# Local attention with v blocks of 80 keys, zero columns around K^T, and new numbers for the issue order

## The chip, the core and the metric

The kernel runs on one core of one Trainium2 chip. A core has five engines that run side by side: TensorE (PE, matrix products; its weight loads are listed as PEld), VectorE (DVE), ScalarE (ACT), GpSimd (POOL) and SyncE (SP), which here only issues transfers. Sixteen DMA engines carry the transfers. The metric is the time of one execution in device microseconds; before the change the median of three runs is 770.74 us (768.55 to 772.76).

## The reference

Two parts. The first is an attention with two terms, over q, k, v of 8 batches, 8 heads, 576 positions and 64 dimensions, in float32:

```python
q_d, k_d, v_d = means over 4 neighbours          # 144 positions instead of 576
out_up = repeat(softmax(q_d k_d^T / 8) v_d, 4)   # the coarse term
mask = |pos_i - pos_j| < 4
out_local = softmax(where(mask, q k^T / 8, -1e9)) v   # each query sees at most 7 keys
x = (out_up + out_local), as 4608 rows of 512
```

The second is a mixture of 8 experts over these 4608 rows: logits `x @ w_gate`, a greedy assignment by sorted logits with at most 576 rows for an expert, then `relu(x w1[e]) w2[e]` for each expert's rows. The change touches the first part alone.

## The kernel before

**Stages.** Stage one computes the attention and the logits. It takes the first 284 us of the profiled span and writes x to DRAM. Stage two finds the fullest expert, gathers its rows, multiplies, and repeats for eight experts. Stage two needs every logit, so it starts when the last unit of stage one has its logits.

**Units.** The local term is worked in 36 units of 128 queries (`u`), each of four windows of 32 queries; a window looks at 38 keys (`KW`), from three before its first query to three behind its last. `loc_s` (L436) makes the scores of a unit on TensorE, one 32x38 product for each window and head, on top of the mask that a first product put there (L428). VectorE takes the maximum and subtracts it (L444, L445), ScalarE makes the exponentials (L446) into a tile `sw` of 64 columns for each head, whose columns 38 to 63 are zero. `loc_t` transposes on TensorE (L454): the two windows of a pair then lie one above the other, the even window's keys on partitions 0 to 63 and the odd window's on 64 to 127. ScalarE copies both halves into the weight tile `pt` (L465, two copies of 64 partitions). `loc_v` (L476) multiplies `pt` with the keys' values `vw`, one product of 128 keys by 64 queries for each pair and head; `norm` (L404 to L407) divides on VectorE. `log_a` (L484) adds the coarse term, `log_t` and `log_m` (L494 to L514) make the logits `lg`.

**Values.** `load_vw` (L229) fills `vw`, one of four buffers: for each window 48 rows of v (`VR`) with all 8 heads, 256 bytes for each row and head. Window 0 of a pair goes to partition 0 and up, window 1 to partition 64 and up, so the six keys that two neighbours share are loaded twice, and 10 more rows come along each time. A window at the end of a batch takes two transfers, of 32 and 6 rows.

**Keys.** The transposed keys `kt` are 576 columns; a window at either end of a batch is pushed inwards (`key0` clamps) and its mask differs.

**The coarse term.** For each batch: `trw` and `trt` transpose q and k (L292, L306), with evacuations (L276 on VectorE, L278 on ScalarE) that `EV` deals out, one in five to VectorE after the first 29 (`EN0`), which alternate. `gsum` makes the sums over four (L265, L268). `down_s`, `down_t`, `down_v` are its scores, transposes and products; its results go to DRAM (`up_dram<-xu`, L387) and come back by `load_up` with each row four times (`up<-up_dram`, L416), which waits until the write has landed.

**What sets the order.** `run` gives every piece a place on one scale, in units, and sorts: `LOC` holds the places of a unit's pieces behind its number, `TW` and `TWS` those of a batch's transposes, `DW` and `DWS` those of its coarse term, `NEXT` those of the loads of a later batch (`q0`, `k0`: the first four heads, `q1`, `k1` the other four, `t` the tail, `v0`, `v1`). The sorted list is what each engine runs, in that order, with no reordering. All loads and stores of stage one go through SP's queue, so a transfer that must wait holds back every later one. `FL`, `FT`, `FD` say how many pieces later some ScalarE and VectorE work is issued. `SETUP` and `SPACE` place the preparation of the routing between the units (L828 to L857).

## Time and profile before

| | before |
|---|---|
| median of three runs | 770.74 us |
| the profiled execution, its own time | 767.14 us |
| its span, first to last instruction | 765.1 us |
| PE busy in the span | 671.1 us (88%) |
| PEld | 464.0 us (61%) |
| DVE | 549.7 us (72%) |
| ACT | 332.8 us (43%) |
| POOL | 235.4 us (31%) |
| mean granted TensorE clock | 0.952 |

The time of the profiled execution is 2.0 us above its span, since the time also holds what lies outside the first and last instruction. Busy shares are means over both stages; stage one is the one to read here, and the windows view gives its share.

### The profile page before, as it was taken

How to read it: one execution, taken by the hardware profiler on the slowest of the kernel's cores; microseconds unless marked ns; L12 is line 12 of the kernel's file. 1: busy time of each engine (PE TensorE's matmuls, PEld its weight loads, DVE VectorE, ACT ScalarE, POOL GpSimd, SP SyncE). 2: the span in 40 equal slices, each digit the busy share in tenths (PEclk: the TensorE clock that was granted, in tenths of full speed). 3: DMA queues.
4: the chain of work that ended last, by engine and by line, in shares of the span. 5: the costliest groups of instructions: out<-in, count | busy, mean ns of one | idle time of the engine just before them, and what ended most of it. 6: DMA issues, size and time to landing. Idle time of an engine off the chain costs nothing.

```text
span 765.1 us, 21134 instructions
## 1 busy us (share of the span) xinstructions
PE 671.1 (88%) x8545; PEld 464.0 (61%) x8545; DVE 549.7 (72%) x1635; ACT 332.8 (43%) x632; POOL 235.4 (31%) x280
## 2 busy tenths in 40 slices
PE   6788998996998963499889799999899999999994
PEld 4667786885877851365356357467466475674852
DVE  4997887887787886788869879899879354361210
ACT  3447766575675540442425325234334244352210
POOL 8173574535436450300400412140220412202011
PEclk9999999998999985599999999999999999999998
DMA  9978999897999750712825645490947733404001
GB/s 283 182 196 243 253 203 255 210 259 222 239 249 233 188 179 1 239 44 93 259 56 221 145 142 183 87 319 2 276 130 264 218 99 114 119 2 106 19 27 35
DMA packets 152900, 126.17 MB, mean 165 GB/s; under 512 B 96996, under 2 KB 127204, under 8 KB 152804
## 3 DMA queue, kind: packets, MB, share of 16 engines
q1 hardware_dynamic: 145424, 103.30, 50.0%
q0 software_dynamic: 6432, 20.98, 8.8%
q8 instruction: 68, 1.11, 0.6%
q10 hardware_dynamic: 948, 0.55, 0.3%
q14 instruction: 28, 0.23, 0.1%
HBM read 95.30 MB, written 21.23 MB: 152 GB/s over the span
## 4 chain that ended last, share of the span: by engine, by line
issue 31%; DVE 24%; PE 22%; DMA 9%; ACT 6%; POOL 5%; SPq 1%; POOLq 0%; ACTq 0%; DVEq 0%
PE pH L1109 4%; PE pX L1138 4%; POOL out_dram L1146 3%; DMA nat<-in_q_dram 2%; DVE cmp L709 2%; PE g L476 2%; PE pR L735 2%; POOL xg L1073 2%; DVE x L407 2%; PE g L292 1%; DMA xt<-xs 1%; ACT pt L465 1%; DMA up_dram<-xu 1%; DVE x L484 1%; ACT qz L278 1%
## 5 line engine op out<-in xcount | busy, mean ns | idle before, releaser
L1109 PE MATMUL pH<-xt,wh 128*128 128x256 f16 (+1 forms) x1024 | 194.5, 288 | 4.7 <-DMA xt<-xs 3.2
L1138 PE MATMUL pX<-wh,ht 128*128 128x512 f16 (+1 forms) x640 | 180.3, 382 | 0.0
L1109 PE MATMUL pH<-xt,wl 128*128 128x320 f16 (+1 forms) x512 | 146.9, 287 | 0.0
L1138 PEld LDWEIGHTS <-ht 128*128 128x128 f16 (+1 forms) x960 | 81.0, 100 | 90.2 <-issue 5.8
L1146 POOL DMA_INDIRECT out_dram<-y,idx x40 | 41.4, 1034 | 276.4 <-ACT y L1143 252.6
L1138 PE MATMUL pX<-wl,ht 128*128 128x512 f16 (+1 forms) x320 | 118.6, 382 | 0.0
L1109 PEld LDWEIGHTS <-wh 128*128 128x128 f16 x1024 | 97.9, 98 | 33.0 <-issue 8.5
L1122 ACT ACTIVATE ht<-pH 128x512 f16<-128x512 f32 (+1 forms) x128 | 45.5, 407 | 117.3 <-PE pH L1109 112.8
L1058 DVE SCALAR_TENSOR_TENSOR wl<-nat,wh 128x512 f16<-128x512 f32 x128 | 85.3, 684 | 2.5 <-ACT wh L1056 0.3
L1125 DVE SCALAR_TENSOR_TENSOR ht<-pH,ht 128x512 f16<-128x512 f32 (+1 forms) x128 | 52.5, 450 | 34.6 <-ACT ht L1122 34.0
L1073 POOL DMA_INDIRECT xg<-x_dram,idx x40 | 42.1, 1053 | 113.3 <-DVE idx L1009 57.6
L1143 ACT ACTIVATE y<-pX 128x512 f32<-128x512 f32 (+1 forms) x40 | 23.8, 594 | 115.7 <-PE pX L1138 71.1
L1056 ACT ACTIVATE wh<-nat 128x1024 f16<-128x1024 f32 x64 | 66.9, 1056 | 6.2 <-DMA nat<-in_moe_w_dram 6.0
L1109 PEld LDWEIGHTS <-wl 128*128 128x128 f16 x512 | 50.2, 98 | 13.0 <-issue 0.6
L465 ACT COPY pt<-g 64x512 f32<-64x512 f32 x72 | 41.7, 579 | 35.5 <-PE g L454 34.3
L1093 DVE SCALAR_TENSOR_TENSOR xs<-xg,xs 128x512 f16<-128x512 f32 (+1 forms) x35 | 23.6, 688 | 45.3 <-ACT xs L1092 44.9
L292 PE MATMUL g<-ident,nat 128*128 128x128 f32 x256 | 40.4, 292 | 8.6 <-DMA nat<-in_k_dram 3.9
L476 PE MATMUL g<-vw,pt 128*64 128x65 f32 x1152 | 45.0, 229 | 2.9 <-ACT pt L465 1.2
L476 PEld LDWEIGHTS g<-vw,pt 128*64 128x64 f32 x1152 | 40.0, 142 | 9.8 <-ACT pt L465 6.2
L278 ACT COPY kt<-g 64x512 f32<-64x512 f32 (+1 forms) x53 | 33.3, 628 | 25.7 <-PE g L292 13.6
L265 POOL TENSOR_TENSOR gtmp<-qz 64x576 f32<-64x576 f32 x28 | 32.0, 1142 | 30.6 <-DVE kdt L268 22.8
L499 DVE SCALAR_TENSOR_TENSOR xt<-g,xt 128x512 f16<-128x512 f32 x36 | 24.6, 685 | 20.2 <-ACT xt L498 20.0
(223 smaller groups left out, 1163.6 us busy)
## 6 DMA issues: line engine op xcount, KB each, us to landing
nat<-in_moe_w_dram SPq DMA_DIRECT2D x28, 1024.0 KB
vw<-in_v_dram SPq DMA_DIRECT2D x136, 96.0 KB
up<-up_dram SPq DMA_DIRECT2D x36, 256.0 KB
x_dram<-x SPq DMA_DIRECT2D x36, 256.0 KB
nat<-in_q_dram SPq DMA_DIRECT2D x16, 512.0 KB
nat<-in_k_dram SPq DMA_DIRECT2D x16, 512.0 KB
nat<-in_v_dram SPq DMA_DIRECT2D x14, 512.0 KB
up_dram<-xu SPq DMA_DIRECT2D x16, 128.0 KB
```

The costliest lines, as they stand in the source:

```text
L278: self.nc.scalar.copy(out, in_)
L292: nc.tensor.transpose(p[:, a, :, fp], src[:, 4 * hh + 2 * a + s, 2 * fp:2 * fp + 2].rearrange("p f d -> p (f d)"), self.ident)
L465: self.nc.scalar.copy(out, in_)
L476: nc.tensor.matmul(o[64 * i:64 * i + 64, 65 * h:65 * h + 65], pt[:, 2 * g + i, h].rearrange("p b q -> p (b q)"), self.vw[u % 4][:, i, 4 * ...
L1056: nc.scalar.activation(hi, r, AF.Copy, scale=sc)
L1058: nc.vector.scalar_tensor_tensor(lo[:, a:a + LOP], r[:, a:a + LOP], sc, hi[:, a:a + LOP], op0=OP.mult, op1=OP.subtract)
L1073: self.fetched = nc.gpsimd.indirect_dma_start(out=xg[:n], out_offset=None, in_=self.x, in_offset=bass.IndirectOffsetOnAxis(ap=idx[:n, c:c ...
L1109: mm = nc.tensor.matmul(p[:, s, :s1 - s0], w[d][a][:, 128 * f:128 * f + 128], xt[:, b, d, s0:s1], start=j == 0, stop=j == len(seq) - 1)
L1122: last = nc.scalar.activation(hi, q, AF.Relu)
L1125: nc.vector.scalar_tensor_tensor(lo, q, 0.0, hi, op0=OP.max, op1=OP.subtract)
L1138: nc.tensor.matmul(p[o:o + m], ht[:, f, h0:h0 + m], w[4 + f // 2][b][:, 512 * (f % 2):512 * (f % 2) + 512], start=j < parts, stop=j >= len ...
L1146: i = nc.gpsimd.indirect_dma_start(out=self.out, in_=y[:n], in_offset=None, out_offset=bass.IndirectOffsetOnAxis(ap=idx[:n, c:c + 1], axis=0))
```

## The change

`load_vw` loads 80 rows for a pair of windows instead of 48 for each; the first block of a batch starts three rows later, the last one is two transfers of 64 and 3 rows. The odd window's keys therefore begin 32 rows below the even window's, and `loc_t` puts them there: its second half is copied to partitions 32 to 95 in two copies of 32 partitions, so three copies on ScalarE instead of two. The rest of `pt` stays zero. `kt` gets three zero columns at each end, in two fixed tiles (`ktp`); `key0` no longer clamps, and the mask excludes the columns outside. The warm-up's tile `wm` now lies in `pt`'s second buffer.

The numbers of the order are new throughout, among them `NEXT`, `TW`, `LOC`, `EV` (one evacuation in four to VectorE instead of one in five, from the 40th on) and `SPACE`.

```diff
--- before.py
+++ after.py
@@ -21,7 +21,7 @@
 QW = 32
 NW = S // QW
 KW = QW + 6
-VR = 48
+VR = 80
 G = S // 4
 
 GM = 128
@@ -32,22 +32,22 @@
 E, F = 8, 1024
 XS = 32.0
 GSN = ('k2',)
-SH1 = 0.416
+SH1 = 0.467
 EARLY = 1
-RDY = -0.651
+RDY = 0.161
 LU = 2
 LA = 3
 LT = 5
-NEXT = (('t', 1.415), ('q0', 1.792), ('k0', 2.351), ('q1', 2.948), ('k1', 2.546), ('v0', 2.861), ('v1', 3.806), ('w', 3.194))
+NEXT = (('t', 1.876), ('q0', 0.674), ('k0', 2.463), ('q1', 2.866), ('k1', 3.746), ('v0', 3.897), ('v1', 3.863), ('w', 3.133))
 FD = 6
 FN = 1
-FL = 7
-FT = 1
+FL = 4
+FT = 0
 PEL = ("s0", "s1", "t", "v0", "v1", "lt", "lm")
-TW = (0.129, 2.439)
-DW = (-0.791, 2.251)
-DWS = {0: (1.96, 3.4), 7: (0.089, 2.426), 2: (0.305, 2.813), 3: (-0.72, 2.467), 1: (-0.345, 2.276), 5: (-0.673, 2.314)}
-LOC = {'up': 1.406, 'st': 4.773, 't': 1.331, 'lm': 7.406, 's0': 0.33, 's1': 0.334, 'lt': 5.423, 'v0': 1.884, 'v1': 1.885, 'add': 4.575}
+TW = (0.129, 2.617)
+DW = (-1.448, 2.214)
+DWS = {0: (1.96, 3.4), 7: (0.089, 2.426), 2: (1.251, 2.601), 3: (-0.348, 2.968), 1: (-0.345, 2.276), 5: (-0.673, 2.314), 6: (-1.824, 1.993)}
+LOC = {'up': 1.395, 'st': 4.914, 't': 1.331, 'lm': 7.649, 's0': 0.33, 's1': 0.334, 'lt': 5.417, 'v0': 1.718, 'v1': 1.803, 'add': 4.664}
 GS1 = ''
 GS0 = 'qk'
 GW = 2
@@ -56,31 +56,31 @@
 UB = 3
 XB = 6
 NPT = 2
-PEV = (0,0)
-EV = (0, 0, 0, 0, 1)
+PEV = (0, 0, 0)
+EV = (0, 0, 0, 1)
 ADDU = 27
 DX = 0
 SETUP = {25:0,35:26}
-SPACE = 0.371
+SPACE = 0.253
 GS = 32.0
-VWT = 1.785
-T0 = (-1.703, 0.95)
-LD0 = (-2.849, -3.627, -0.654, -0.8, 0.549)
-LD1 = (0.094, -1.118, -0.846, -0.839, -0.245, 0.414, 2.297, 2.161)
-TWS = {1: (1.746, 2.94), 6: (0.447, 2.327)}
-E0 = -0.295
-E1 = 2.863
-UE = 31
-CE = 0.101
+VWT = 1.976
+T0 = (-1.695, 2.143)
+LD0 = (-3.332, -4.99, -0.667, -0.921, 0.832)
+LD1 = (0.255, -1.073, -1.273, -0.839, -0.661, 0.459, 1.648, 2.161)
+TWS = {1: (1.853, 2.764), 6: (0.536, 2.453), 3: (-0.024, 2.685)}
+E0 = -3.356
+E1 = 4.638
+UE = 35
+CE = 0.554
 NWARM = 13
 EV0 = (0, 1)
-EN0 = 29
+EN0 = 39
 TB = 3
-SUM0 = (1.042, 1.417, 1.097)
+SUM0 = (0.827, 1.133, 2.137)
 
 
 def key0(w):
-    return min(max(QW * w - 3, 0), S - KW)
+    return QW * w - 3
 
 
 def ukind(u):
@@ -106,15 +106,13 @@
         self.ident, ident = ident
         identh = cst.tile([128, 130 + H], BF, name="identb")
         self.identb, self.half, self.own8 = identh[:, :128], identh[:, 128:130], identh[:, 130:]
-        self.wm = cst.tile([128, 128], BF, name="wm")
-        nc.vector.memset(self.wm, 1.0)
         self.mask = cst.tile([128, 4, 4 * KW], BF, name="mask")
         self.wgf = cst.tile([128, 4, E], F32, name="wgf")
         self.wg16 = cst.tile([128, 4, 2, E], F16, name="wg16")
         for t, src in ((self.ident, ident), (identh, identb), (self.mask, maskc)) + tuple(more):
             nc.scalar.dma_start(t, src)
         self.wg = wg
-        self.vw, self.vd, self.qz, self.qdz, self.qdt, self.sw, self.ptw = [], [], [], [], [], [], []
+        self.vw, self.vd, self.qz, self.qdz, self.qdt, self.sw, self.ptw, self.ktp = [], [], [], [], [], [], [], []
         self.sd = cst.tile([128, 9, G], F32, name="sd")
         self.sdt = cst.tile([128, 2 * H, GT], F32, name="sdt")
         for i in range(2):
@@ -123,12 +121,15 @@
 
 
             self.vd.append(cst.tile([128, 2, H, D + 1], F32, name=f"vd{i}"))
+            self.ktp.append(cst.tile([128, HP, S + 6], F32, name=f"kt{i}"))
         for i in range(4):
             self.vw.append(cst.tile([128, 2, H, D + 1], F32, name=f"vw{i}"))
         for i in range(NSW):
             self.sw.append(cst.tile([128, H, 64], F32, name=f"sw{i}"))
         for i in range(NPT):
             self.ptw.append(cst.tile([128, 4, 4, 2, QW], F32, name=f"pt{i}"))
+        self.wm = self.ptw[1][:, 0, 0].rearrange("p b q -> p (b q)").bitcast(BF)
+        nc.vector.memset(self.wm, 1.0)
 
     def gate(self):
         nc = self.nc
@@ -152,6 +153,9 @@
             heads(nc.vector, nc.vector, self.qdt[0])
             for t in self.vd:
                 nc.vector.memset(t[:, 0, :, D:], 1.0)
+            for t in self.ktp:
+                nc.vector.memset(t[:, :, :3], 0.0)
+                nc.vector.memset(t[:, :, S + 3:], 0.0)
             for t in self.sw:
                 nc.gpsimd.memset(t[:, :, KW:], 0.0)
             nc.gpsimd.memset(self.ptw[0], 0.0)
@@ -220,14 +224,13 @@
     def load_vw(self, u):
 
         nc, src = self.nc, self.v
-        for c in range(4):
-            b, w = divmod(4 * u + c, NW)
+        for c in range(2):
+            b, w = divmod(4 * u + 2 * c, NW)
             k0 = key0(w)
 
-            for r0, n in ((0, VR),) if k0 + VR <= S else ((0, 32), (32, KW - 32)):
-                p0 = 64 * (c % 2) + r0
+            for r0, n in ((3, VR),) if w == 0 else ((0, VR),) if k0 + VR <= S else ((0, 64), (64, 3)):
                 nc.sync.dma_start(
-                    self.vw[u % 4][p0:p0 + n, c // 2, :, :D],
+                    self.vw[u % 4][r0:r0 + n, c, :, :D],
                     bass.AP(tensor=src.tensor, offset=src.offset + (b * H * S + k0 + r0) * D,
                             ap=[[D, n], [S * D, H], [1, D]]))
 
@@ -279,7 +282,7 @@
 
     def dest(self, b):
         if b not in self.kt:
-            self.kt[b] = self.wk.tile([128, HP, S], F32, name="kt")
+            self.kt[b] = self.ktp[b % 2][:, :, 3:3 + S]
         return self.kt[b]
 
     def trw(self, b, which, hh, s):
@@ -434,7 +437,7 @@
             for a in range(4):
                 h = 4 * g + a
                 nc.tensor.matmul(sv[32 * a:32 * a + 32, 4 * g + c], self.qz[b % 2][:, h // 2, h % 2, QW * w:QW * w + QW],
-                                 self.kt[b][:, h // 2, key0(w):key0(w) + KW], start=False, stop=True,
+                                 self.ktp[b % 2][:, h // 2, QW * w:QW * w + KW], start=False, stop=True,
                                  skip_group_check=True, tile_position=(0, 32 * a))
         if g == 0:
             return
@@ -454,9 +457,9 @@
             nc.tensor.transpose(p[:, 128 * i:128 * i + 128], t[:, 2 * i:2 * i + 2].rearrange("p h k -> p (h k)"),
                                 self.ident)
         out = self.ptw[u % NPT]
-        for a in range(2):
-            r = slice(64 * a, 64 * a + 64)
-            self.pevac(a, out[r, :, :, a], p[r].rearrange("p (i h q) -> p i h q", h=4, q=QW))
+        for j, (a, r0, n) in enumerate(((0, 0, 64), (1, 64, 32), (1, 96, 32))):
+            d0 = r0 - 32 * a
+            self.pevac(j, out[d0:d0 + n, :, :, a], p[r0:r0 + n].rearrange("p (i h q) -> p i h q", h=4, q=QW))
 
     def pevac(self, a, out, in_):
         if PEV[a]:
@@ -1234,7 +1237,8 @@
         for c in range(4):
             w = (4 * u + c) % NW
             d = QW * w + p[:, None] % QW - key0(w) - np.arange(KW)[None]
-            m[kind, c][np.abs(d) < 4] = 0.0
+            k = key0(w) + np.arange(KW)[None]
+            m[kind, c][(np.abs(d) < 4) & (k >= 0) & (k < S)] = 0.0
     base, at = [], -32768
     for (_, step), (n, nxt) in zip(LV, LV[1:] + ((1, 0),)):
         at -= step
```

What the new numbers move is shown at three places. Lines of the new kernel stand three lower down from `load_nat` on, so L229 becomes L232 and L465 becomes L468.

SP's queue, around the results of the third batch's coarse term (`xu`); `nat` are the loads of q, k and v for a later batch. Before:

```order
L387 DMA up_dram<-xu 128x256
L394 DMA up_dram<-xu 8x16x64
L215 DMA nat<-in_k_dram 128x4x256
L487 DMA x_dram<-x 128x512
L416 DMA up<-up_dram 128x1x512 x2
L215 DMA nat<-in_v_dram 128x4x256
L215 DMA nat<-in_q_dram 128x4x256
L206 DMA natw<-in_v_dram 128x1x256
L229 DMA vw_129<-in_v_dram 48x8x64 x4
L416 DMA up<-up_dram 128x1x512
L487 DMA x_dram<-x 128x512
L215 DMA nat<-in_v_dram 128x4x256
```

After:

```order
L219 DMA nat<-in_k_dram 128x4x256
L419 DMA up<-up_dram 128x1x512 x2
L219 DMA nat<-in_q_dram 128x4x256
L490 DMA x_dram<-x 128x512
L232 DMA vw_129<-in_v_dram 80x8x64 x2
L210 DMA natw<-in_v_dram 128x1x256
L419 DMA up<-up_dram 128x1x512
L219 DMA nat<-in_k_dram 128x4x256
L219 DMA nat<-in_v_dram 128x4x256 x2
L490 DMA x_dram<-x 128x512
```

The second half of q stood behind half of v and stands ahead of it now; the second half of k stood ahead of the two `up` loads and stands behind three of them; both halves of v are last.

ScalarE, the last units of stage one. Before:

```order
L446 ACTIVATE sw_131<-sw_131 128x8x38
L465 COPY pt_133<-g 64x16x32 x2
L498 ACTIVATE xt<-g 128x512
L446 ACTIVATE sw_132<-sw_132 128x8x38
L465 COPY pt_134<-g 64x16x32 x2
L498 ACTIVATE xt<-g 128x512 x5
```

After:

```order
L449 ACTIVATE sw_131<-sw_131 128x8x38
L468 COPY pt_133<-g 64x16x32
L468 COPY pt_133<-g 32x16x32 x2
L501 ACTIVATE xt<-g 128x512
L449 ACTIVATE sw_132<-sw_132 128x8x38
L468 COPY pt_134<-g 64x16x32
L468 COPY pt_134<-g 32x16x32 x2
L501 ACTIVATE xt<-g 128x512 x5
```

The copies into `pt` are three where they were two; what stands around them is the same.

VectorE, the preparation of the routing between the last units (`am`, `oh`). Before:

```order
L444 TENSOR_REDUCE mx<-g 128x8
L445 TENSOR_TENSOR sw_132<-g,mx 128x8x38
L850 TENSOR_REDUCE am<-eq 128x26
L514 TENSOR_REDUCE lg<-g 128x8
L499 SCALAR_TENSOR_TENSOR xt<-g,xt 128x512
L857 TENSOR_TENSOR oh<-eq,amu 128x8x26
L404 TENSOR_SCALAR den<-g 128x4
L405 RECIPROCAL den<-den 128x4
L407 TENSOR_TENSOR x<-g,den 128x256
```

After:

```order
L853 TENSOR_REDUCE am<-eq 128x26
L407 TENSOR_SCALAR den<-g 128x4
L408 RECIPROCAL den<-den 128x4
L410 TENSOR_TENSOR x<-g,den 128x256
L407 TENSOR_SCALAR den<-g 128x4
L408 RECIPROCAL den<-den 128x4
L410 TENSOR_TENSOR x<-g,den 128x256
L860 TENSOR_TENSOR oh<-eq,amu 128x8x26
L447 TENSOR_REDUCE mx<-g 128x8
```

`am` and `oh` stood behind the last unit's scores (`mx`, `sw`); they stand ahead of them now, about a unit earlier.

## The prediction

> **What bounds the kernel now.** I read the windows view first, to see where the span goes and which stage the edited lines are in, then who waited for whom, then the chain of waits, then groups, transfers and the timeline of single places.
>
> The windows view: start:end, length, busy us of PE, PEld, DVE, ACT and POOL with instructions, granted clock, share of the DMA engines, GB/s.
>
> ```profile
> 0.00:284.00 284.00, 244.70 (x5164) 202.35 (x5165) 230.73 (x620) 170.13 (x333) 150.32 (x198) 0.96 0.89 228
> 120.00:130.00 10.00, 7.50 (x147) 6.42 (x144) 6.71 (x17) 8.50 (x18) 3.28 (x4) 0.94 0.98 249
> 130.00:140.00 10.00, 9.76 (x196) 8.47 (x196) 7.94 (x23) 5.39 (x10) 3.14 (x6) 0.89 0.93 213
> 180.00:190.00 10.00, 5.17 (x103) 3.97 (x101) 6.16 (x16) 5.38 (x13) 3.94 (x5) 0.84 0.79 231
> 190.00:200.00 10.00, 10.00 (x176) 9.15 (x175) 4.98 (x14) 6.79 (x13) 2.43 (x3) 0.82 1.14 300
> 220.00:230.00 10.00, 8.55 (x198) 7.41 (x197) 7.64 (x23) 9.73 (x21) 0.00 (x0) 1.00 1.12 277
> 284.00:765.00 481.00, 426.40 (x3384) 261.61 (x3383) 318.92 (x1016) 162.62 (x299) 85.10 (x82) 0.95 0.43 128
> ```
>
> Stage one, the attention, is 284 us; the other 481 us hold none of the edited lines and stay. In stage one PE is busy for 86%, DVE for 81%, the DMA engines for 89%: three resources near their limit, none at it throughout. So a saving on one counts only where that one is late, and two windows show where: in 120 to 130 and 180 to 190 both PE and DVE sit idle. The waits (total us, times, longest) of the attention name the cause:
>
> ```profile
> PE g L306 <- DMA natt<-in_k_dram: 4.6, 2, 3.9
> PE g L292 <- DMA nat<-in_k_dram: 3.9, 2, 3.3
> PE g L292 <- DMA nat<-in_q_dram: 3.2, 3, 2.3
> DVE x L484 <- DMA up<-up_dram: 2.6, 3, 1.7
> PEld g L476 <- ACT pt L465: 6.2, 14, 0.9
> ```
>
> The chain of waits (start, length, what) shows how the two idle stretches come about:
>
> ```profile
> 113.38 4.45 DMA up_dram<-xu
> 117.84 0.56 SPq L416
> 118.46 0.60 SPq L416
> 119.11 0.59 SPq L215
> 119.73 8.35 DMA nat<-in_q_dram
> 128.22 0.63 PE g L292 x4
> ...
> 177.75 5.92 DMA up_dram<-xu
> 183.74 0.56 SPq L416
> 184.34 4.22 DMA nat<-in_k_dram
> 188.69 1.09 PE g L292 x4
> ```
>
> A write of the coarse term must land before SP may issue the loads that read it back; the next batch's q or k is queued behind, lands 4.2 to 8.4 us later, and PE waits for it. These are stalls of the transfer path, and they cost clock too: 0.89 and 0.82 in the windows after them.
>
> **What the change takes off the transfers.** Before, a batch's windows bring 17 x 48 + 38 = 854 rows of v; now 8 x 80 + 67 = 707. Times 8 heads and 8 batches that is 9,408 packets of 256 bytes fewer, 2.41 MB. SP issues 152 transfers for them before, by the view of the tile `vw`, and 80 now:
>
> ```profile
> L229 SPq DMA_DIRECT2D vw<-in_v_dram x152: 311/466/2377, 12.8 to 266.5; - x152
> q1 hardware_dynamic: 100272, 63.57, 86.8%
> q1 hardware_dynamic: 4673, 2.07, 80.3%
> ```
>
> At the median of 466 ns the 72 issues are 33.6 us of SP's time. The two `q1` rows (packets, MB, share of 16 engines) are SP's queue in 0 to 285 us and in 250 to 260 us, where 4,156 of the packets are under 512 bytes. The first gives 0.868 x 285 x 16 / 100,272 = 39.5 ns for a packet, or by bytes 3,958 us x 2.41 / 63.57; the second 0.803 x 160 / 4,673 = 27.5 ns. So the saving of queue time is between 150 / 16 = 9.4 us by bytes and 9,408 x 39.5 ns / 16 = 23.2 us by mean packets. I take 16.2 us from the second row, whose packets are the kind that goes. That is a twentieth of the queue's time, spread over the stage.
>
> **What of it reaches the end.** At most what the stalls cost: idle PE in the two windows, 2.5 + 4.8 = 7.3 us; lost clock, 7.50 x 0.06 + 9.76 x 0.11 + 5.17 x 0.16 + 10.00 x 0.18 = 4.2 us; DVE's waits for `up`, 2.6 us; together 14.1 us. At least nothing, if another wait stands right behind. The 4.6 us for the first `natt` stay, since nothing ahead of it in SP's queue changes. Both stalls open with a transfer, and the reordering helps the first: q's second half, late at 119.73, no longer stands behind half of v. It doesn't help the second, where k's first half still stands behind the `up` loads. I take 9 us, nearer the upper end. That order can also cost is the third rival.
>
> A rule of the skill bears on the clock part. The Trainium skill, "TensorE: Matmul & The Clock Gate", section "What's actually happening", says that an idle window of some 3.4 us throttles the PE clock to half and that about as much sustained work restores it. The trace agrees in kind, with 0.84 and 0.82 around the wait of some 4 us. By that rule a stall cut below the window would give back the whole 4.2 us, and the term would be some 11 us instead of 9.
>
> **What it adds on ScalarE and VectorE.**
>
> ```profile
> L465 ACT COPY pt<-g 64x512 f32<-64x512 f32 x72 | 41.7, 579 | 35.5 <-PE g L454 34.3
> L278 ACT COPY kt<-g 64x512 f32<-64x512 f32 x46 | 28.9, 627 | 14.2 <-PE g L292 13.6
> L276 DVE COPY qz<-g 64x512 f32<-64x512 f32 x26 | 17.9, 689 | 2.5 <-PE g L292 2.1
> ```
>
> The 36 more copies into `pt` have as many elements for each partition, so I take the same 579 ns: 20.8 us of ACT. `EV` moves 11 evacuations from ACT to DVE: 11 x 627 ns = 6.9 us off ACT, 11 x 689 ns = 7.6 us onto DVE. Net ACT +13.9 us, DVE +7.6 us. Most of this is covered: ACT is busy for 60% of the stage, and where it is full, as in 220 to 230 (9.73 of 10), DVE has slack (7.64), which is where evacuations happen. If DVE's cover were gone all 7.6 us would show; I take 1 us. The zero columns are four small memsets behind a memset of 2 us; the last POOL memset of `pt` must now wait for the warm-up, whose products end at 1.21 + 5.24 = 6.45 us, 0.25 us after it is due, and POOL idles 0.64 us later on for the first v:
>
> ```profile
> 1.21 5.24 PE L617 MATMUL g<-wm 128*128 128x512 bf16 x13 [1.21 <-DVE wm L110]
> 6.20 0.95 POOL L160 MEMSET pt<- 128x1024 f32 x1
> 15.64 1.27 POOL L241 TENSOR_TENSOR gtv<-nat 128x512 f32<-128x512 f32 x1 [0.64 <-DMA nat<-in_v_dram]
> ```
>
> So nothing for these. What isn't covered is the delay of `pt` itself. One unit at the end of the stage, from the timeline:
>
> ```profile
> 266.47 0.66 PE L454 MATMUL g<-ident,sw 128*128 128x128 f32 x4
> 267.22 1.18 ACT L465 COPY pt<-g 64x512 f32<-64x512 f32 x2 [1.64 <-PE g L454]
> 268.45 1.22 PE L476 MATMUL g<-vw,pt 128*64 128x65 f32 x32
> ```
>
> The value products start 0.05 us after the second copy. PE has about 1.3 us of other work between (scores, logits, a transpose of x), just enough for two copies, not for three. So such a unit grows by nearly 0.58 us. In the new order nine units after the first have only this work between `loc_t` and `loc_v`, among them the last four; before it was 15, so the order makes room elsewhere. Upper bound 9 x 0.58 = 5.2 us, lower bound the last four, 2.3 us, where nothing else is left to do. I take 3.5 us.
>
> **The end of stage one.** Two steps of the routing's preparation stand on DVE among the last units:
>
> ```profile
> 272.30 0.50 DVE L850 TENSOR_REDUCE am<-eq 128x26 f32<-128x208 bf16 x1
> 273.45 0.97 DVE L857 TENSOR_TENSOR oh<-eq,amu 128x208 bf16<-128x208 bf16 x1
> ```
>
> DVE runs without a gap there until the last unit is normalized. Moved a unit ahead, to where PE will be waiting for the third copy, they leave up to 1.4 us; I take 1 us, nothing being the other end.
>
> **Sum.** -9 + 1 + 3.5 - 1 = -5.5 us. The profiled execution's own time is 767.14 us with a span of 765.1 us, so 761.6 and about 759.6 us now. It is 3.6 us below the median of 770.74 us, so as a median 765.2 us; I say 765.
>
> **Rivals.**
>
> *The transfers were hidden anyway.* When PE and DVE no longer wait for q and k they wait for each other: 86% and 81% busy in a chain that goes back and forth leaves little slack. For it: explicit waits for these loads are only 7.1 us. Against it: the two idle windows with both engines below 7.6 of 10. Then the transfer term is 4 us, and -4 + 1 + 3.5 - 1 leaves 770.
>
> *The 80-row block runs unevenly.* Blocks of 48 rows alternate between the lower and the upper 64 partitions; 64 of the 80 rows are in the lower half. If each half has its own way in and both halves work at once, the busier half carries 72 x 64 rows now against 72 x 48 before, a third more. v's 54,656 packets at 27.5 ns are 94 us of queue time, so +31 us instead of -16. The queue, at 86.8%, would be full, and the stalls grow: +9 in place of -9, and 783. Against it: the two queue rows price a packet by its number more than by its bytes (27.5 ns where nearly all are of 256 bytes, 39.5 ns at a mean of 634), which points at the engines and not at the ways into the memory. The Trainium skill, "SBUF — State Buffer", section "Door 1: The DMA port swizzle (why `[64,N]` ≈ `[32,N]`)", states such halves: partitions 0 to 63 reach 8 of 16 ports. No row here shows ports.
>
> *The last loads come too late; this one ends slower.* On the order's scale a load leads its first use by 4.5 plus the place of the transpose minus the place of the load. For k's first half that is 2.53 units before (4.5 + 0.386 - 2.351) and 2.44 now; for k's second half 3.62 before (4.5 + 1.669 - 2.546) and 2.54 now (4.5 + 1.788 - 3.746). A unit is 284 / 36 = 7.9 us, so the second half of k comes 8.5 us later, behind three `up` loads. It then has the lead with which the first half already waited 3.3 us. If it waits as long in three of six batches, with 2.1 us of clock each, that is 16 us; with the 9 us won and 3.5 us as above the result is 781. It decides as soon as k lands later than 2.5 units after its issue. Against it: q's halves both gain lead, and everything ahead of k in the queue is shorter.
>
> **Chances.** Forecast 0.48, with a range of its own from 758 to 769 (transfer term from 14 to 5 us); hidden transfers 0.27; late k 0.19; uneven blocks 0.06. A measurement of this kernel tells a change from none at about 0.5%, 3.9 us. Faster by more than that: nine tenths of the first case and a tenth of the second, 0.46. Slower: three quarters of the third, the fourth, and a fifth of the second, 0.25. The rest, 0.29, is no change. The range goes from 756, the whole of the stalls and a little more with an order that also closes gaps elsewhere, to 779, most of the late-k case.
>
> **What would show it.** The queue's packets in stage one should fall by 9,408 and its share to about 0.82; SP should issue 80 `vw` transfers. PE in the windows of the third and fifth coarse terms should lie above 9 of 10, and the waits of L295 (now L292) for q and k should fall below 3 us in total. The waits for `pt` on PEld should rise from 6.2 to about 10 us, and the last units should be 0.5 us longer each. I am wrong if stage one ends after 284 us: then either L295 waits for k's second half, or `pt` waits are twice what I took.

## The result, and the profile after

The changed kernel takes 776.37 us (median of 6 runs, 775.04 to 781.85) against 769.27 us of the kernel before beside it (764.84 to 772.76): a ratio of 1.011 with an interval of 1.0063 to 1.0157. It is slower, where 765 us and a small gain were forecast. Ratios here and below are taken from fast executions alone, since some executions of a kernel run in a slower state, so a ratio need not be the quotient of the two medians. Its profiled execution took 776.55 us with a span of 774.9 us.

The windows view of the changed kernel, with the columns and most of the stretches quoted of the kernel before:

```profile
0.00:284.00 284.00, 241.94 (x5161) 203.01 (x5162) 241.25 (x632) 183.15 (x358) 148.95 (x198) 0.96 0.83 219
120.00:130.00 10.00, 9.66 (x201) 7.89 (x202) 8.53 (x24) 8.10 (x19) 3.75 (x5) 1.00 1.08 295
180.00:190.00 10.00, 8.62 (x184) 7.01 (x185) 9.69 (x23) 6.11 (x15) 7.33 (x10) 1.00 0.96 256
284.00:774.00 490.00, 427.66 (x3384) 261.89 (x3383) 319.14 (x1019) 163.11 (x299) 90.19 (x82) 0.94 0.44 125
```

The two idle stretches have filled up, at full clock (7.50 and 5.17 us of PE before, at 0.94 and 0.84). Yet stage one is not shorter: the last logits of the attention end at 284.38 us, 0.51 us later than before. The other 9 us are in stage two, whose work is the same (3,384 products in both) but which now needs 490 us in place of 481. SP's queue up to 285 us (packets, MB, share of 16 engines) and SP's issues of v (shortest, median and longest in ns, first to last) show that the transfers did what was foreseen:

```profile
q1 hardware_dynamic: 89688, 61.16, 81.4%
L232 SPq DMA_DIRECT2D vw<-in_v_dram x80: 319/567/2712, 11.1 to 264.1; - x80
```

The waits of stage one (total us, times, longest) name what took their place. The k and q transposes (L295) wait 0.6 us for `nat` on PE, where it was 7.1 us, and TensorE waits for the weights and for the normalization instead:

```profile
PEld g L479 <- ACT pt L468: 9.8, 13, 1.4
PE g L479 <- ACT pt L468: 8.3, 13, 1.3
PE g L497 <- DVE den L407: 5.4, 4, 2.1
```

The groups with their shapes show the price of the third copy (count, total us, mean ns):

```profile
L468 ACT COPY pt<-g 32x512 f32<-32x512 f32 x72 | 41.6, 577 | 1.7
L468 ACT COPY pt<-g 64x512 f32<-64x512 f32 x36 | 20.8, 578 | 36.7 <-PE g L457 36.4
```

Half as many partitions cost the same time. The timeline of one of the last units, whose counterpart the prediction quotes with two copies in 1.18 us:

```profile
265.98 1.78 ACT L468 COPY pt<-g 64x512 f32<-64x512 f32 x3 [1.56 <-PE g L457]
...
267.81 1.15 PE L479 MATMUL g<-vw,pt 128*64 128x65 f32 x32 [0.74 <-ACT pt L468]
```

The value products stand still for 0.74 us.

**Where stage two loses.** Counted from the start of the first gather of x rows, the first piece `xs` of the second, third and fourth expert comes 4.5, 6.0 and 9.0 us later than before, and the end 9.3 us. So the loss arises at three places: at the first gathers, and at those of the second and third expert. The first place, on GpSimd's timeline before (start, length):

```profile
312.13 1.69 POOL L1073 DMA_INDIRECT xg<-x_dram,idx  x1 [29.37 <-DVE used L964]
314.12 1.48 POOL L1073 DMA_INDIRECT xg<-x_dram,idx  x1 [0.30 <-issue]
```

and in the changed kernel:

```profile
312.62 6.47 POOL L1076 DMA_INDIRECT xg<-x_dram,idx  x1 [29.35 <-DVE used L967]
319.38 0.95 POOL L1076 DMA_INDIRECT xg<-x_dram,idx  x1 [0.30 <-issue]
```

The first gather takes 4.8 us longer and the second 0.5 us less, so the third starts 4.3 us later. VectorE at that moment, before:

```profile
311.83 0.15 DVE L964 TENSOR_TENSOR used<-used,code 128x1 f32<-128x1 f32 x1
312.06 0.69 DVE L1058 SCALAR_TENSOR_TENSOR wl<-nat,wh 128x512 f16<-128x512 f32 x1
```

and in the changed kernel:

```profile
312.31 0.15 DVE L967 TENSOR_TENSOR used<-used,code 128x1 f32<-128x1 f32 x1
312.38 0.68 DVE L1061 SCALAR_TENSOR_TENSOR wl<-nat,wh 128x512 f16<-128x512 f32 x1
...
313.80 3.69 DVE L1061 SCALAR_TENSOR_TENSOR wl<-nat,wh 128x512 f16<-128x512 f32 x6
317.41 0.66 DVE L814 TENSOR_TENSOR lm<-lg,pen 128x288 f32<-128x288 f32 x1
```

VectorE splits the first expert's weights (`wl`) in one unbroken run up to 318.07 us, and the gather, which reads its indices from SBUF on GpSimd, ends 1.02 us later. In both kernels the run overlaps the gathers, but before, `wl` started 0.23 us after `used` and now 0.07 us after it. The order of VectorE's instructions, with what each waits for, gives the likely reason, which was not tested apart: `kt` left the pool of work tiles, the tiles behind it moved, and `wl`'s buffer no longer lies over tiles whose loads seven DMA semaphores tell of. Six of its waits are gone (numbers of buffers and semaphores left out; before, then now):

```
L1058 SCALAR_TENSOR_TENSOR wl<-nat,wh 128x512 [waits DMAHW3,DMAHW4,DMAHW2,DMAHW5,DMAHW1,DMAHW7,DMAHW0,Activation]
L1061 SCALAR_TENSOR_TENSOR wl<-nat,wh 128x512 [waits DMAHW7,Activation]
```

At the other two places the transposes by DMA (`xt<-xs`) land late. ScalarE prepares the pieces `xs` in two buffers, so the third piece waits for the first transpose. First and third piece of the second expert before:

```profile
374.68 0.63 ACT L1092 ACTIVATE xs<-xg 128x512 f16<-128x512 f32 x1 [2.16 <-DMA xg<-x_dram,idx]
380.09 0.63 ACT L1092 ACTIVATE xs<-xg 128x512 f16<-128x512 f32 x1 [3.31 <-DVE nj L751]
```

and in the changed kernel:

```profile
379.63 0.63 ACT L1095 ACTIVATE xs<-xg 128x512 f16<-128x512 f32 x1 [1.78 <-DMA xg<-x_dram,idx]
388.17 0.63 ACT L1095 ACTIVATE xs<-xg 128x512 f16<-128x512 f32 x1 [6.25 <-DMA xt<-xs]
```

5.41 us between them before, 8.54 now. By the times of the transfers, a packet of the queue q8 falls among these transposes now and fell among the gathers before. Its 67 packets carry 1.10 MB, 16 KB each:

```profile
q8 instruction: 67, 1.10, 0.7%
```

That is TensorE's program: 17,335 instructions, some 256 to a packet, and 17,379 before. The 44 are instructions that only wait: 285 before and 241 now by the traces, 232 with the data part of the change alone (e_blocks below) and 289 with the order's numbers alone (e_order). So it is the data part that shortens the program. 44 instructions out of the 256 of a packet move every later packet against the work.

### The profile page after: what moved, and what is told of

Its sections match the earlier page's. It is cut to its first block, busy times and chain, and to the rows that moved or that the text cites. A ratio compares the mean times of both kernels' runs of the same rounds, so it can differ in the third digit from the quotient of the medians.

```text
span 774.9 us, 21066 instructions
## 1 busy us (share of the span) xinstructions
PE 669.6 (86%) x8545; PEld 464.9 (60%) x8545; DVE 560.4 (72%) x1650; ACT 346.3 (45%) x657; POOL 239.1 (31%) x280
## 4 chain that ended last, share of the span: by engine, by line
issue 30%; DVE 12%; PE 12%; POOL 5%; DMA 3%; ACT 1%; POOLq 0%; ACTq 0%; DVEq 0%
PE pH L1112 4%; PE pX L1141 4%; POOL out_dram L1149 3%; DMA xt<-xs 2%; DVE cmp L712 2%; POOL xg L1076 2%; PE pR L738 2%; DMA xg<-x_dram,idx 1%; DVE wl L1061 1%; DVE ht L1128 1%; DVE xs L1096 1%; PE pR L747 0%; DVE ohl L999 0%; DVE m L831 0%; PE pR L752 0%
## 5 line engine op out<-in xcount | busy, mean ns | idle before, releaser
L1076 POOL DMA_INDIRECT xg<-x_dram,idx x40 | 47.5, 1187 | 110.0 <-DVE idx L1012 55.5
L468 ACT COPY pt<-g 32x512 f32<-32x512 f32 (+1 forms) x108 | 62.4, 578 | 38.4 <-PE g L457 36.4
L295 PE MATMUL g<-ident,nat 128*128 128x128 f32 x256 | 39.5, 285 | 1.4 <-issue 0.8
L439 PE MATMUL g<-kt,qz 128*32 128x38 f32 x2304 | 36.4, 205 | 4.0 <-DVE kt L279 2.2
L281 ACT COPY qz<-g 64x512 f32<-64x512 f32 (+1 forms) x54 | 34.4, 636 | 9.8 <-PE g L295 6.4
```

The source lines that it names most:

```text
L295: nc.tensor.transpose(p[:, a, :, fp], src[:, 4 * hh + 2 * a + s, 2 * fp:2 * fp + 2].rearrange("p f d -> p (f d)"), self.ident)
L439: nc.tensor.matmul(sv[32 * a:32 * a + 32, 4 * g + c], self.qz[b % 2][:, h // 2, h % 2, QW * w:QW * w + QW], self.ktp[b % 2][:, h // 2, QW ...
L468: self.nc.scalar.copy(out, in_)
L1076: self.fetched = nc.gpsimd.indirect_dma_start(out=xg[:n], out_offset=None, in_=self.x, in_offset=bass.IndirectOffsetOnAxis(ap=idx[:n, c:c ...
```

## The experiments

Fourteen kernels were run. Each time stands beside the kernel before on the same chip (769.59, 767.55, 768.12 and 776.67 us in the four groups of the table). Stage two is the profile's length from the first gather's start to the end; the last columns are that gather's length and, for the second expert, the start of the q8 packet and of the third and fifth `xs`, all in us from the first `xs`.

```
run             median  ratio to before           stage two  gather   q8  third fifth
before (first)  -       -                         453.0      1.69   -2.7  5.41 10.39
e_before2       768.08  one execution             452.6      1.68   -2.6  5.38 10.39
after (first)   776.37  1.0110 [1.0063, 1.0157]   462.3      6.47   +4.4  8.54 14.18
e_after2        781.56  1.0147 [1.0092, 1.0202]   463.4      6.46   +3.6  8.09 13.69
e_blocks        788.11  1.0191 [1.0118, 1.0265]   464.7      6.47   +5.3  7.81 13.67
e_order         774.06  1.0020 [0.9975, 1.0066]   450.0      1.68   -2.9  5.58 10.60
e_gap           776.11  1.0103 [1.0067, 1.0139]   459.6      1.70   +4.5  8.03 13.77
e_late_gather   767.31  0.9991 [0.9960, 1.0021]   453.5      1.31   -2.6  7.42 12.98
e_pe_pad        778.16  1.0104 [1.0069, 1.0140]   458.3      6.46   -2.8  5.48 10.99
e_pe_shift      771.62  1.0070 [1.0036, 1.0104]   459.6      1.68   +4.0  8.36 13.91
e_two_copies    771.91  1.0051 [1.0021, 1.0081]   461.1      6.47   +4.9  7.74 13.42
e_three_copies  780.67  1.0175 [1.0125, 1.0225]   451.8      1.68   -2.8  5.58 10.62
e_copy_dve      802.17  1.0426 [1.0380, 1.0473]   460.8      6.47   -2.9  5.50 10.60
e_long_run      791.64  one execution             469.9      8.88   +4.6  7.58 13.29
e_no_run        775.96  0.9993 [0.9958, 1.0027]   460.3      1.45   +3.8  7.46 12.24
```

**Both kernels again, and the change in two halves.** The data part alone (e_blocks) and the numbers of the order alone (e_order):

```diff
 e_blocks: before, and
-VR = 48
+VR = 80          (load_vw, ktp, the mask and the three copies of loc_t with it)
 e_order: before, and
-NEXT = (('t', 1.415), ...
+NEXT = (('t', 1.876), ...          (with all other numbers of the change but VR and PEV)
```

> The kernel before, unchanged, profiled once more. Stage one ended at 283.7 us in its first profile (last logits of the attention), the first gather of stage two took 1.69 us from 312.13, and the whole 767.14 us. Theory A (stage two is delayed in the changed kernel by a shift of its instruction or weight transfers that is fixed by the program): again 766 to 768 us, first gather 1.5 to 2 us, stage two (from last logits to the end) within 1 us of 481 us. Theory B (the delays of stage two come and go from one execution to the next): first gather or the transposes of stage two longer than in the first profile, 770 us or more. Theory C (the edits of stage one cost the time) says nothing of this run beyond stage one at 284 us.

> The changed kernel, unchanged, profiled once more. In its first profile stage one ended at 284.2 us (0.5 us later than before), the first gather took 6.47 us from 312.62, and the whole 776.55 us. Theory A: the same again, first gather 6 to 7 us, the transposes of the second expert late, stage two 8 to 10 us longer than before, 776 us. Theory B: first gather back at 1.7 us or the later transposes back, whole 768 to 772 us in this profile. Theory C: stage one ends later than in the kernel before by about the whole difference, 290 us or more, which the first profile already speaks against.

> Only the data part of the change: blocks of 80 keys, zero columns, masks and three copies of the weights, with the order's numbers of before. Theory A (stage one is even, stage two moves by a shift of its transfers): stage one 281 to 287 us; the end anywhere from 764 to 778 us, and what differs from stage one lies at the first gather and at the transposes of stage two. Theory C (the blocks with their third copy cost the time): stage one longer than 286 us, the whole 774 to 780 us. My prediction's transfer term alone would give 765 to 768 us.

> Only the order's numbers of the change, with blocks of 48 keys, the old K^T and two copies of the weights. Theory A: stage one 284 to 290 us since the numbers fit other blocks, the end set by stage two as in the other kernels. Theory C': the order costs the time, k's second half late behind three loads of the coarse term as my third rival had it: waits of the q and k transposes for their loads over 10 us in stage one (7.1 us before), the whole 775 to 785 us. If the blocks alone cost it, this kernel stays at 768 to 772 us.

Stage two's loss is fixed by the program: 452.6 to 453.0 us twice before, 462.3 and 463.4 us twice after. So theory A holds for its 10 us, and B falls. But A said that stage one is even in every kernel, and that fell: stage one ended at 284.4 and 291.8 us in two executions of one kernel, so a single profile tells nothing of it below some 7 us, and only timed ratios are used for it here. From 1.0191 x 769.59, e_blocks is 14.7 us slower (9.1 to 20.4), of which stage two has 11.9 (464.7 less the 452.8 of before); e_order is 1.5 us slower (-1.9 to 5.1) although its stage two is 2.8 us shorter. By these middles each half loses 3 to 4 us in stage one, which the two together don't; the intervals are wider than that for e_blocks. Both delays of stage two come with the data part: the first gather takes 6.47 us and the packet is late in e_blocks, and neither in e_order. e_order has the longest waits for k of these kernels, though its expectation was over 10 us for q and k:

```profile
PE g L292 <- DMA nat<-in_k_dram: 6.0, 3, 3.6
```

These are 3.9 us before and nearly gone in the changed kernel. The third rival's late k appears only where the blocks of v are the old ones.

**The gather and VectorE's run.** In e_gap a tiny product stands ahead of `wl` in the changed kernel; in e_late_gather GpSimd copies some indices ahead of the gather in the kernel before:

```diff
 e_gap: after, and
             nc.vector.tensor_tensor(self.used, self.used, code, op=OP.add)
+            if first:
+                for _ in range(3):
+                    nc.vector.tensor_tensor(rr, es, rem, op=OP.mult)
 e_late_gather: before, and
+        if first:
+            with self.tc.high_priority():
+                nc.gpsimd.tensor_copy(idx[64:, 4:5], idx[64:, 3:4])
```

> The changed kernel with three tiny repeats of an 8-element product on VectorE, the first of them ahead of the first `wl` of stage two, so that this `wl` starts some 0.2 us later; nothing else differs. Theory P: what starts first wins. In before the first gather starts 0.07 us after `wl` and takes 1.69 us, in the changed kernel 0.24 us after it, and ends only 1.0 us after VectorE's unbroken run of `wl` and `lm` (6.47 us). With `wl` back at or behind the gather's start the gather should take 1.5 to 2 us, and the whole falls by 4 to 5 us against the changed kernel, to about 773 us where that stands at 776 to 781. Rival Q (the 6.47 us come from a code load or from the memory's layout): still 6.4 to 6.5 us, the whole unchanged.

> The kernel before with one copy of 64 unused indices on GpSimd ahead of the first gather, so that the gather starts 0.2 to 0.4 us later against VectorE's `wl`; nothing of stage one differs. Theory P: the gather is shut out until VectorE's run ends, takes 5.5 to 6.5 us in place of 1.69, and the whole is 4 to 5 us longer, 773 to 775 us against 769. Rival Q: the gather keeps its 1.7 us, the whole 769 to 770.

The first gather of e_gap was back at 1.70 us, but the second was caught:

```profile
318.84 1.70 POOL L1079 DMA_INDIRECT xg<-x_dram,idx  x1 [29.37 <-DVE rr L970]
320.84 4.46 POOL L1079 DMA_INDIRECT xg<-x_dram,idx  x1 [0.30 <-issue]
...
323.86 0.66 DVE L814 TENSOR_TENSOR lm<-lg,pen 128x288 f32<-128x288 f32 x1
```

It ended at 325.30, 0.78 us after VectorE's run (323.86 + 0.66), so the 4 to 5 us that were expected back did not come. In e_late_gather nothing was caught, though the gather began 0.45 us after `wl`:

```profile
314.56 0.69 DVE L1058 SCALAR_TENSOR_TENSOR wl<-nat,wh 128x512 f16<-128x512 f32 x1
...
315.01 1.31 POOL L1076 DMA_INDIRECT xg<-x_dram,idx  x1 [0.93 <-DMA nat<-in_moe_w_dram]
```

So "who starts first wins" is refuted as a rule for this kernel. Two further runs asked whether the run sets the length at all. e_long_run repeats the last `wl` piece twice (four products more); e_no_run has no `wl` on VectorE there and the old length of TensorE's program:

```diff
 e_long_run: after, and
-            for a in range(0, 1024, LOP):
+            for a in (0, LOP) + (0, LOP) * 2 * (first and k == 3):
 e_no_run: after with the 22 tiny products of e_pe_pad, and
+            if first and k < 4:
+                nc.scalar.activation(lo, r, AF.Copy, scale=0.0)
+                w[k] = (hi, lo)
+                return
```

> The changed kernel with the last `wl` piece of the first expert computed twice more (four more products of 0.6 us on VectorE, right behind the others and ahead of `lm`), nothing else. Theory P' (GpSimd cannot read the indices while VectorE works without a gap, so the first gather ends about 1.0 us after the last operation of that run, whichever began first): VectorE's run ends 2.4 us later and the gather takes 8.8 to 9.0 us in place of 6.47. Rival Q (its length is its own, a code load or a fixed delay): 6.4 to 6.5 us.

> The changed kernel without the low parts of the first expert's first weights: ScalarE writes zeros for them in place of VectorE's eight `wl` (so the output lacks that part), and 22 tiny products behind the warm-up give TensorE's program the length of before. Both causes that I see in stage two are then gone. Theory P' and F together: first gather at most 1.7 us, second at most 1.5 us, third `xs` of the second expert 5.4 to 5.6 us behind the first, stage two from the first gather to the end 451 to 454 us (453.0 and 452.6 before, 462 to 463 in the changed kernel), and the whole within 3 us of before, 767 to 772 us. Rival: another 3 us or more of stage two have a cause not found: 456 us or more from the first gather.

```profile
319.77 8.88 POOL L1076 DMA_INDIRECT xg<-x_dram,idx  x1 [29.36 <-DVE used L967]
...
326.98 0.66 DVE L814 TENSOR_TENSOR lm<-lg,pen 128x288 f32<-128x288 f32 x1
```

The run ends at 327.64 and the gather at 328.65, 1.01 us later; in the changed kernel it was 1.02. The length is a wait for VectorE. Stage two is 6.5 to 7.6 us longer than in the changed kernel, though; 2.4 us of it are the gather, and the rest is not explained (the kernel before is also 7 to 9 us slower on that chip than on the others). Without the `wl` the first two gathers are short:

```profile
323.47 1.45 POOL L1082 DMA_INDIRECT xg<-x_dram,idx  x1 [29.37 <-DVE used L969]
325.22 0.96 POOL L1082 DMA_INDIRECT xg<-x_dram,idx  x1 [0.30 <-DVE eq L847]
```

VectorE works without a gap there too, but on other operations:

```profile
323.23 0.67 DVE L816 TENSOR_TENSOR lm<-lg,pen 128x288 f32<-128x288 f32 x1
323.81 0.19 DVE L964 TENSOR_TENSOR n<-n,am 128x36 f32<-128x36 f32 x1
323.93 0.66 DVE L833 TENSOR_REDUCE m<-lm 128x36 f32<-128x288 f32 x1
```

The gather ends at 324.92, 1.02 us after `lm` and not after `m`, so not every unbroken stretch of work on VectorE shuts it out, as theory P' had it. The whole is level with before: 0.9993 (0.9958 to 1.0027). But this run is no clean sum of the two causes. VectorE has eight operations of 0.7 us less ahead of `lm`. The q8 packet was to go and fell among the transposes again, at +3.8 us, with the third `xs` at 7.46 us in place of 5.4 to 5.6. And stage two took 460.3 us, not 451 to 454, in an execution that was 9.5 us above the median.

**The instruction packet.** Tiny products behind the warm-up bring TensorE's program back to its old length in the changed kernel (e_pe_pad), or give the kernel before the changed one's phase (e_pe_shift, 17,591 = 17,335 + 256):

```diff
             self.nc.tensor.matmul(p, w, w[:, None].to_broadcast([128, 4, 128]), start=True, stop=True)
+        for _ in range(22):          (e_pe_pad, after; 106 in e_pe_shift, before)
+            self.nc.tensor.matmul(p[:, :16], w, w[:, :16], start=True, stop=True)
```

> The changed kernel with 22 tiny products (44 instructions on TensorE) behind the warm-up, which gives TensorE's program the length it had before. Theory F: the first transposes of the second and third expert land late (7 us in place of 4) because a 16 KB instruction packet of TensorE (the queue q8) now falls among them, and before it fell among the gathers, 5 us earlier. With the old length it goes back: no q8 packet within the first 6 us of these transposes, the third `xs` of the second expert 5.4 us behind the first in place of 8.5, the whole 3 to 5 us shorter than the changed kernel. Rival G (the transposes are late because they meet the gathers in another phase): the packet moves and the transposes stay late, the whole unchanged or up to 1 us longer for the products at the start.

> The kernel before with 106 tiny products (212 instructions) behind the warm-up: TensorE's program has the changed kernel's phase within a packet of 256 instructions. Theory F: the q8 packet falls among the transposes of the second and third expert, the third `xs` of the second expert comes 8 us or more behind the first (5.4 us before), and the whole is 3 to 5 us longer, of which up to 1 us may be the products at the start, where TensorE waits for its first loads to 11.6 us anyway: 772 to 775 us. Rival G: stage two keeps its times, the whole 769 to 771 us.

The pieces of e_pe_pad, 5.48 us apart:

```profile
388.33 0.63 ACT L1097 ACTIVATE xs<-xg 128x512 f16<-128x512 f32 x1 [2.23 <-DMA xg<-x_dram,idx]
393.81 0.63 ACT L1097 ACTIVATE xs<-xg 128x512 f16<-128x512 f32 x1 [3.38 <-DMA xt<-xs]
```

and of e_pe_shift, 8.36 us apart:

```profile
380.90 0.63 ACT L1094 ACTIVATE xs<-xg 128x512 f16<-128x512 f32 x1 [1.68 <-DMA xg<-x_dram,idx]
389.26 0.63 ACT L1094 ACTIVATE xs<-xg 128x512 f16<-128x512 f32 x1 [6.22 <-DMA xt<-xs]
```

The packet moved as foreseen and the transposes with it, in both directions. Stage two of e_pe_pad is 4.0 to 5.1 us shorter than the changed kernel's. The whole was to be 3 to 5 us shorter, and the timed ratios, 1.0104 against 1.0110 and 1.0147, do not show that; they are uncertain by 3 to 4 us each. e_pe_shift is 5.4 us slower than before (2.8 to 8.0). Its stage two is longer by 6.8, but not all by the packet: its second gather took 4.42 us and ended 0.78 us after VectorE's run, in a kernel with the old blocks. And e_late_gather has a late third piece (7.42 us) with no q8 packet there. At the second expert another thing separates the runs without this exception: the fourth of the expert's gathers starts 0.12 to 0.51 us behind the first `xs` in all nine with a late third piece and 0.03 to 0.33 us ahead of it in the seven others, so that whether the packet acts directly or through the gathers' phase stays open there. At the third expert that phase is alike (0.56 to 0.76 us, but for e_three_copies), and the packet still tells: the third `xs` comes 7.54 to 9.11 us behind the first with a packet 4.5 to 5.5 us behind it, and 6.11 to 7.40 us without.

**The third copy.** e_two_copies takes it from the changed kernel, e_three_copies adds it to the kernel before, e_copy_dve gives it to VectorE:

```diff
 e_two_copies: after, and
-        for j, (a, r0, n) in enumerate(((0, 0, 64), (1, 64, 32), (1, 96, 32))):
+        for a in range(2):          (the old copies of 64 partitions each)
 e_three_copies: before, and
-        for a in range(2):
+        for a, r0, n in ((0, 0, 64), (1, 64, 32), (1, 96, 32)):
 e_copy_dve: after with 42 tiny products, and
-PEV = (0, 0, 0)
+PEV = (0, 0, 1)
```

> The changed kernel with two copies of 64 partitions in place of three per unit; the odd half of the weights then stands in the old layout, so the value products work on wrong rows of v, with the same number of instructions but for 36 copies on ScalarE. Theory S (the third copy eats what the transfers give): TensorE's waits for `pt` fall from 18 us (8.3 and 9.8 on the two parts of the engine) to about 8 us as in before (1.2 and 6.2), and stage one, with it the whole, gets 4 to 8 us shorter than the changed kernel: 770 to 773 us, with stage two as long as in the changed kernel (462 to 464 us from the first gather). Rival T (the chain between the engines is full anyway; another wait takes the place): `pt` waits fall but the whole stays within 2 us of 776 to 779. My prediction's term was 3.5 us for the copy.

> The kernel before with three copies per unit in the old layout (64, 32 and 32 partitions), nothing else. Theory S: waits for `pt` rise by 8 us or more, the whole 4 to 8 us longer: 772 to 776 us. My prediction's bounds of 2.3 to 5.2 us would give 770 to 773. Rival T: within 2 us of before, since the old order has more work between the transposes and the value products (24 units of 36 have over 28 rows there).

> The changed kernel with the third copy on VectorE beside ScalarE's second, and 42 tiny products behind the warm-up that give TensorE's program the length of before (so no instruction packet among the transposes of stage two). Theory S: the copies take two lengths again, `pt` waits fall by 6 us or more, stage one 2 to 6 us shorter than the changed kernel; with the 4 us of the packet 767 to 772 us. Rival T: VectorE, with 25 us more work at 85% busy, becomes the bound of stage one, which is 5 us or more longer: 778 to 785 us.

TensorE's waits for `pt` up to 285 us, all of them in e_two_copies:

```profile
PEld g L479 <- ACT pt L468: 2.9, 7, 0.9
```

in e_three_copies:

```profile
PEld g L476 <- ACT pt L465: 15.6, 20, 1.3
PE g L476 <- ACT pt L465: 10.7, 14, 1.1
```

and in e_copy_dve:

```profile
PEld g L479 <- DVE pt L466: 30.9, 22, 6.9
PE g L479 <- DVE pt L466: 27.7, 20, 6.7
```

The products of e_two_copies work on wrong rows of v, in the same number. Without the third copy the waits are nearly gone and the whole is 3.9 us above before (1.6 to 6.2); stage two has 8.3 of that (461.1 less 452.8), so stage one is 4.4 us shorter than before. With the copy in the kernel before it is 13.4 us longer (9.6 to 17.3), all of it in stage one: theory S, and more than any of my numbers. The copy on VectorE is the worst of all, 32.7 us slower than before with 8.0 of that in stage two, beyond both expectations: TensorE waits up to 6.9 us at a time for it.

e_later_values sets the value products later:

```diff
 e_later_values: after with 8 tiny products, and
-LOC = {... 'v0': 1.718, 'v1': 1.803, ...}
+LOC = {... 'v0': 2.2, 'v1': 2.285, ...}
```

> The changed kernel with the value products due 0.48 of a unit later in the order, so that more other work stands between the transposes and them in 20 of 36 units, and 8 tiny products behind the warm-up that give TensorE's program the length of before. Theory S: `pt` waits fall by 4 us or more and stage one gets 2 to 5 us shorter; with the 4 us of the packet 768 to 773 us. Rival T: the wait goes elsewhere (the normalization and the transposes of x come later), stage one as long as in the changed kernel or longer: 773 to 778 us.

It took 1087.88 us. Its value products wait for loads of v, here up to 400 us; in no other run is this over 4 us in all:

```profile
PE g L479 <- DMA vw<-in_v_dram: 173.4, 26, 13.9
```

The products seem to have moved behind the next load into their own buffer, so that they work on v of a later unit and the attention is not the reference's. It says nothing of S or T.

## Why the prediction was wrong

**The step that failed** is the first paragraph's "the other 481 us hold none of the edited lines and stay". They held none and grew by 9.5 and 10.6 us in two profiles. 4.3 us are the first gather, shut out by VectorE's run, less what the second gives back. 4.0 to 5.1 us go with the place of TensorE's instruction packets, by what e_pe_pad gives back. The two make 8.3 to 9.4 us, which leaves 1.2 us without a name. No timed ratio shows the two taken away together.

**The transfers.** The step was right as far as the queue: 80 issues, a share of 81.4% where some 82% were foreseen, and 10,584 packets fewer. 9,408 were foreseen for the rows of v; the other 1,176 carry almost no bytes (2.41 MB went in all) and come to 16 for each of the 72 transfers that went, with 24 over. Of queue time, 0.868 x 285 x 16 less 0.814 x 285 x 16 is 246 us, 15.4 us of each engine, against 16.2. What of it reaches the end was mis-sized. Terms of -9, +1 and -1 without the copy should have left stage one 9 us shorter; e_two_copies shows 4.4 (2.1 to 6.7). One part of the term that failed is the clock. 4.2 of its at most 14.1 us were clock, which the rule of the Trainium skill cited there would give back whole. In the two windows the clock did rise to 1.00, but over stage one it is 0.96 in both kernels and 0.95 in e_two_copies, since other windows of the changed kernel lost it:

```profile
20.00:30.00 10.00, 6.76 (x117) 5.88 (x116) 9.28 (x24) 2.19 (x4) 1.81 (x3) 0.66 1.16 235
40.00:50.00 10.00, 7.34 (x71) 6.42 (x75) 7.14 (x18) 4.61 (x11) 6.76 (x12) 0.77 0.39 102
80.00:90.00 10.00, 8.24 (x198) 6.96 (x198) 9.62 (x26) 5.24 (x11) 9.22 (x13) 0.83 0.77 217
```

These were 0.83, 1.00 and 1.00 before. Nor do filled windows show that the saving arrived. In e_three_copies, with the old blocks and a queue share of 85.9%, PE is busy for 8.89 and 7.86 us in the two windows and its q and k transposes wait 0.3 us for `nat`, though no transfer was taken away. Where the other half of the gain went is not shown: the 5.4 us for `den` are 0.2 us in e_two_copies. In size it is the first rival, whose term was 4 us, and its sum of -0.5 us for stage one is what the changed kernel shows there: 8.5 us (1.0110) less 9.5 and 11.3 us (1.0147) less 10.6 leave -1.0 and +0.7 us, each some 4 us uncertain.

**The third copy.** 3.5 us was taken, with bounds of 2.3 and 5.2. The changed kernel's -1.0 and +0.7 us less e_two_copies' -4.4 make it 3.4 to 5.1, with some 4 us of uncertainty: right in size. 0.58 us for each copy and some 10 us of `pt` waits on PEld came out at 0.58 and 9.8. Not seen was that TensorE itself would wait 13 times, not nine, for 8.3 us. Nor what e_three_copies shows, that 36 more copies cost some 14 us in the kernel before. Whether its order or its blocks of 48 rows make that difference is not shown: with the old order and the new blocks, e_blocks has a stage one that is 2.8 us longer (-2.8 to 8.5), copies and fewer transfers together.

**The other rivals.** The uneven blocks are refuted by the queue's share, which fell as it should with even ones. The late k is refuted for the changed kernel, where L295 waits 0.6 us for k; the order alone has it. The sign to look for, "wrong if stage one ends after 284 us", came true by 0.4 us, which tells nothing where two executions of one kernel differ by 7 us. PE in the second window reached 8.62 us, where above 9 was foreseen.

The Trainium skill, "SBUF — State Buffer", section "SBUF: two separate sides", calls the port pair that VectorE and GpSimd share an exclusive lock: a VectorE operation with two SBUF inputs against a GpSimd operation that reads SBUF, whichever starts first, blocks the other for the whole instruction. The caught gathers agree that it is a full block and not a slowdown. Here it lasted for a whole run of instructions rather than one, and the gather of e_late_gather, which started second, got through; the measurement decides. The same page, section "A bandwidth-pool intuition that's wrong (but worth ruling out)", has a transfer issued by GpSimd blocked until about 115 ns after VectorE's end; these gathers end 0.78 to 1.02 us after it, and no row shows where in them the wait ends. The Trainium skill, "Runtime: NRT & Kernel Launch", section "Instruction fetch mechanics", has programs refilled in blocks of 16 KiB at a cost that is mostly hidden. TensorE's packets agree in size; their place is not free of cost here: the third `xs` came 8.54 us behind the first and 5.48 in e_pe_pad, 5.41 and 8.36 in e_pe_shift.

No run beat the kernel before by more than its interval.

## What to carry to other kernels

Work that is not edited can still change its time: a program's length sets where its instruction packets fall, and an edit elsewhere can take waits off an instruction, here most likely through the place of its buffer. So time the untouched stages apart before an edit is blamed or praised. Idle windows that fill do not show that a saving on transfers reached the end; here about half of it did. A split copy costs its full length again, and its price depends on the kernel around it: 36 more copies cost some 4 us in one and 14 in the other.

## What was not expected of the hardware

An indirect gather on GpSimd that normally takes 1.3 to 1.7 us took 6.47 us, and 8.88 us when VectorE's run of `wl` was 2.4 us longer. It ended 1.01 to 1.02 us after that work when it was the first gather, 0.78 us when it was the second. What decides whether a gather is caught stays open: e_pe_shift's second gather began 0.64 us into the run of six `wl` and took 4.42 us, and the kernel before, with the same 0.64 us, took 1.48. One 16 KB packet of TensorE's program among the DMA transposes goes with 2 to 3 us more between the first and the third piece of the second expert. The packet itself, in the changed kernel's transfers from 383 to 385 us (packets, MB, share of 16 engines), took 4.5% of 2 us x 16, or 1.4 us of one engine:

```profile
q8 instruction: 1, 0.02, 4.5%
```

Why more than that is lost was not tested.
